# Attention and SwiGLU in one kernel: who makes which sum when

## The chip, the cores and the metric

The kernel runs on one NeuronCore of a Trainium2 chip. Its engines work side by side, each through its own queue in order: TensorE (PE) multiplies, VectorE (DVE), ScalarE (ACT) and GpSimd (POOL) work on elements, and SyncE (SP) issues nearly all DMA transfers. The metric is the device time of one execution in microseconds, as the median of several runs.

## The reference

Two blocks in a row. All arithmetic is in f32; the four FFN weights are handed over in f64.

```python
q_n, k_n = rmsnorm(q, g_q), rmsnorm(k, g_k)          # 8 batches, 12 heads, 448 x 64
scores = q_n @ k_n.T / sqrt(64)
attn = exp(scores - max) / (sum + 1e-9)
x = (attn @ v)   # heads side by side: 3584 tokens x 768
xn = x / sqrt(mean(x * x) + 1e-6) * rms_g
out = (silu(xn @ w_gate) * (xn @ w_val)) @ w_out     # 768 -> 1536 -> 768
```

## The kernel before

**Tiling.** Attention goes by pairs of heads: g runs from 0 to 47, six pairs to each of the eight batches b. While pair g's scores, exponentials and weighted values are made, the FFN of the batch before is fed in between them in small items. The program is written out by hand in order: `pe(fn)` emits one step of TensorE work, counts it in `now["t"]`, and then emits what was put off with `after(n, fn)` to that step. `fill()` takes FFN items from `todo`, as many as are due by cost, and after each emits side work on VectorE: a weight conversion (`convert`), a left sum (`slow`, `first_sums`), and sums of weights (`derive`, `derive_o`, `derive_q`). So an instruction's place in its engine's queue is set by the step in which it was emitted.

**FFN as fast matrix products.** Batch 0 multiplies plainly (`plain`, L1590) while the f64 weights are converted to f32 in 72 pieces; each piece passes through load, `split` (two ScalarE instructions, L907 and L908), `join` (three VectorE instructions, L913 to L915), an add on GpSimd (L964) and a store to DRAM (L952). From batch 1 on, gate and value products use a scheme of 15 products in place of 18 for each 2x3 by 3x3 block product (`PRODUCTS`, `product`, matmuls at L1182), in four groups of columns (`GROUPS`). Its left operands are sums of x (`LEFT_G`), its right operands are raw weight blocks (b11 to b33) or combined ones (v1 to v14, `RIGHT_G`). Nine combined blocks per group, 36 in all, are made once, during batch 1, by `derive` with one or two VectorE instructions each (L1087, L1090), used at once, and stored to DRAM, from where later batches load them. Twenty-four sums of output weights (`derive_o`, L1122) and 21 sets of further sums (`derive_q`, L1150 to L1153) are made beside it in batches 1 and 2. For batches 2, 5 and 6 the output projection (`out_quads`, L1518) runs a scheme of products inside products; its left sums are made by `left_q1` (L1392) and `left_sums` (L1364).

**Places.** Weight blocks live in one arena of 66 units: blocks of four units for gate and value ("wg"), of three for the output weights ("w"). Batch 1's gate blocks ("wg1") can also lie in six buffers that the conversion no longer needs. While sets of `derive_q` are outstanding, 18 units are set apart for the blocks that `derive_o` and `derive_q` read. `ask` walks the list of loads in order and issues the next one only if more than `keep_free` places would be left: six for batch 1's gate blocks, three otherwise, one around the first gate blocks of batch 2. `derive` needs one place for its result and its sources loaded some steps before. If a product's combined block is not there, `fill` forces the sum first. `block` picks the place that was freed longest ago, the lowest at a tie. `give_back` frees a place one step after its last use, three steps for "wg1".

**The steps that the change touches.**

- Pair 7 (g == NPAIR + 1) opens the overlapped part. `rms_x(0)` sums squares over x with four small matmuls (L726), after GpSimd's last addition (L644), and takes the root on VectorE and GpSimd (L728, L730). `norm_x(0)` spreads the result over partitions (L738) and scales the six chunks of x (L744).
- In each later even pair, the first step begins with `totals(g - 1)`: matmuls for the softmax denominators (L692), copies on ScalarE (L696, L699), reciprocals on VectorE. Its banks come from the same set of four as those of the scores (L659).
- `norm_x(b)` puts its six scalings off to later steps: two to a step, three in batch 1.
- In q1, the tenth product of a group, batches 2, 5 and 6 make three of the left sums of their output projection (`left_q1`) in the last group.

The lines of `ask` and `block` at issue are these:

```python
            kind, keep_free = "wg" if key[0] == "wg" else "w", 3
            if key[1] == 1 and key[0] == "wg":
                kind, keep_free = "wg1", 6
...
        span = min(places(kind), key=lambda span: (max(freed[i] for i in span), span[0]))
```

Of the kernel before, what the change touches and what calls it, by code (L numbers as in the profile page):

```python
# [18 lines left out]
B, H, S, D = 8, 12, 448, 64  # L19
# [316 lines left out]
def safe_scores(  # L336
# [37 lines left out]
    st = {}  # L374
# [4 lines left out]
    def after(n, fn):  # L379
        due.append((now["t"] + n, fn))  # L380
# [351 lines left out]
    def norm_x(b):  # L732


        rs = st.pop(("rx", b))
        ps = (ps_s if b else ps_f).tile([128, 512], F32, name="rb", tag="s" if b else "f")
        for t in range(NT):
            nc.tensor.transpose(ps[:, t * P:(t + 1) * P], rs[:, t:t + 1].to_broadcast([P, 128]), ident[0:P, 0:P])  # L738

        whole = st["x", b]  # L740

        def scale(hp):
            x = whole[:, hp, :]
            nc.vector.scalar_tensor_tensor(x, x, rg[:, hp:hp + 1], ps[:, 0:S], ALU.mult, ALU.mult)  # L744

        for hp in range(NPAIR):
            if b:
                after(hp // (3 if b == 1 else 2), lambda hp=hp: scale(hp))
            else:
                scale(hp)  # L750
        if b == 0:
            return

        parts = st.pop(("x", b)).rearrange("p (h c) n -> p h c n", h=2)
        a = st["left", b] = {f"a{i + 1}{k + 1}": parts[:, :, k, i * HT:(i + 1) * HT] for i in range(2) for k in range(3)}

        def place(name):
            if name in OVER:
                return a[OVER[name]]
            if name in MADE[:4]:  # L760
                t = s_pool.tile([128, S], F32, name="xs")
            elif name in ("S2", "S0"):
                t = l2_pool.tile([128, S], F32, name="l2")
            else:
                t = more_x[("S4", "S5", "S13").index(name)]
            return t.rearrange("p (h n) -> p h n", h=2)

        def op(name):
            first, second, what = LEFT_G[name]
            one, two = a[first], a[second]  # L770
            a[name] = place(name)
            nc.vector.tensor_tensor(a[name], one, two, what)

        slow.extend((name, lambda name=name: op(name)) for name in MADE)
        st["x_at"] = now["t"]
# [88 lines left out]
        return [span for span in spans if None not in [freed[i] for i in span]]  # L864

    def block(kind="w"):
        span = min(places(kind), key=lambda span: (max(freed[i] for i in span), span[0]))
        for i in span:
            freed[i] = None
        if span[0] in spare:  # L870
            return spare[span[0]], span
        return arena[:, span[0] * 128:span[-1] * 128 + 128], span
# [165 lines left out]
    def ask():  # L1038

        if turn_of["n"] < TURNS:  # L1040
            return
        while side and (room(1, "side") or side[0][0] == "wd" and asked["derived"] > 32 and room(4, "wg")):
            key = side.pop(0)
            asked[key] = now["t"]
            st[key] = block("side" if room(1, "side") else "wg")
            nc.sync.dma_start(out=data(key), in_=home(key))
        while asked["n"] < len(uses):
            key = uses[asked["n"]]
            kind, keep_free = "wg" if key[0] == "wg" else "w", 3
            if key[1] == 1 and key[0] == "wg":  # L1050
                kind, keep_free = "wg1", 6
            elif asked["derived"] < len(derived):
                return
            elif asked["n"] in next_gate:
                keep_free = 1
            if key[0] == "wo" and key[2][0] == "T" and ("kept", *key[2:]) not in asked:
                return
            if key[0] == "wq" and asked.get("sums_q", 0) < KG * (key[2] + 1):
                return
            if not room(keep_free + 1, kind):  # L1060
                return
            asked["n"] += 1
            asked[key] = now["t"]
            st[key] = block(kind)
            src = home(key)
            nc.sync.dma_start(out=data(key)[:, 0:src.shape[-1]], in_=src)
# [103 lines left out]
        after(3 if key[0:2] == ("wg", 1) else 1, ask)  # L1170


    def product(b, g, left, right, onto=None):

        a = st["left", b]
        while left not in a:
            slow.pop(0)[1]()
        bank = ps_f.tile([128, 512], F32, name="ff", tag="f") if onto is None else onto
        key = ("wg", b, g, right)
        for w in range(2):  # L1180
            for c in range(2):
                nc.tensor.matmul(bank[:, w * HT:(w + 1) * HT], lhsT=data(key)[:, (2 * w + c) * 128:(2 * w + c + 1) * 128],  # L1182
                                 rhs=a[left][:, c, :], start=onto is None and w == c == 0, stop=c == 1, skip_group_check=True)
        done_with(key)
        return bank

    def three(b, n):
# [11 lines left out]
        def plus(name, ps):  # L1199
            nc.vector.tensor_tensor(T[name], ps[:, 0:S], T[name], ALU.add)  # L1200
# [56 lines left out]
        def q7(make):  # L1257
            onto("c11", make(bank["B"]), "d", ALU.subtract)

        def q2(make):  # L1260
            plus("c11", make(bank["X"]))

        def q0(make):
            onto("c23", make(bank["Y"]), "s")

        def q1(make):
            plus("c21", make(bank["B"]))
            if n == len(GROUPS) - 1 and in_quads(b):
                left_q1(b, 0, range(3))

        def q14(make):
            plus("c12", make(bank["X"]))
# [355 lines left out]
    LEFT = 10  # L1628
    todo, part = [], {"all": 0.0, "spent": 0.0, "slot": 0, "slots": 1}

    def fill(n=None):

        if n is None:
            part["slot"] += 1
            upto = part["all"] * min(part["slot"] / part["slots"], 1.0)
            n = 0
            while n < len(todo) and part["spent"] + todo[n][0] / 2 < upto:
                part["spent"] += todo[n][0]
                n += 1
        for _ in range(min(n, len(todo))):  # L1640
            _, turns, sums_made, fn = todo.pop(0)
            while turn_of["n"] < turns:
                if not convert():
                    pe(idle)
            made, key = sums_made or (0, None)
            while asked["derived"] < made or (key and key not in st):
                before = dict(asked)
                derive(0)
                if key and key[0] == "wo":
                    derive_o(0)  # L1650
                ask()
                if before == asked:
                    pe(idle)
            pe(fn)
            convert()

            if first_sums:
                first_sums.pop(0)()
            elif slow and now["t"] != st.get("no_x") and now["t"] - st["block"] > 4 and now["t"] - st["x_at"] >= NPAIR and may_make(slow[0][0]):
                slow.pop(0)[1]()  # L1660
            if 2 < now["t"] - st["block"] < 5:
                derive()
            if now["t"] - st["block"] > 4 and now["t"] != st.get("left_sums"):
                made = 0
                while made < 2:
                    done = derive()
                    if not done:
                        break
                    made += done
                for _ in range(0 if made else 2):  # L1670
                    derive_o()
                derive_q()

    def idle():
        pass
# [101 lines left out]
    for g in range(NG + 1):  # L1777
# [51 lines left out]
        if g == NPAIR + 1:  # L1829
            some = lambda *parts: [exps(g, i, scores(g, i)) for i in parts]  # L1830
            pe(lambda: (rests(g), some(0, 1)))
            pe(lambda: rms_x(0))
            pe(lambda: values(g - 1))
            pe(lambda: some(2, 3))
            pe(lambda: norm_x(0))
            pe(lambda: some(4, 5))
            pe(lambda: sums(g - 1))
            later_sums(g, 2)
            begin(0, 15)
        else:  # L1840
            sums_due = g % 2 == 0
            pe(lambda: (totals(g - 1) if sums_due else None, step(g, 0)))
            pe(lambda: [step(g, i) for i in (1, 2)])
            pe(lambda: [step(g, i) for i in (3, 4)])
            pe(lambda: ([step(g, i) for i in (5, 6)], weigh(g - 1, 2) if sums_due else hold(g - 1)))
            if g < NG:
                later_sums(g, 2)
        st["block"] = now["t"]
        after(2, lambda g=g: load_v(g + 2))
        if hp:  # L1850
            fill()
            norm_k(g + 1, 0)
            squares(g + 2, 0)
            squares(g + 2, 1)
            pe(lambda: turn(g + 1, 0))
            norm_k(g + 1, 1)
            some_rests(g)
            fill()
            pe(lambda: turn(g + 1, 1))
            fill()  # L1860
            continue
        fill(3)
        norm_k(g + 1, 0)
# [53 lines left out]
```

## Time and profile before

| | |
|---|---|
| median of 3 runs | 1528.84 us (1526.25 to 1530.41) |
| the profiled execution | 1526.52 us, its span 1524.7 us |
| granted TensorE clock | 0.994 in the mean |
| busy: ACT, POOL | 604, 741 us |
| DMA, mean | 212 GB/s |
| matmuls of the gate and value products, the largest group | 254.0 us in 1272 instructions of 353 ns |
| sums of exponentials on GpSimd (L714) | 253.1 us in 205 instructions of 1235 ns |

"Busy" is the time in which an engine has an instruction running. A row of the timeline or of the groups names the line, the engine, the operation, the tile written and those read, the shape and a count; what stands in brackets is the idle time of the engine just before it and the instruction that ended that idle time. PEld is the weight load, which runs beside the matmuls. The granted clock is 1.00 at full speed.

### The profile page before, as it was taken

What the parts mean: (1) busy time and instruction counts of PE and PEld (TensorE: products, weight loads), DVE (VectorE), ACT (ScalarE), POOL (GpSimd) and SP (SyncE); (2) the same over time, 40 slices, a digit from 0 to 9 for tenths busy, and PEclk for the clock granted to TensorE, in tenths of its full rate; (3) what the DMA queues carried; (4) which work ended last, traced back from release to release, by engine and by line L of the source; (5) the groups of instructions that cost most, each with busy time, mean ns of one, the idle gap of its engine ahead of it and who ended that gap; (6) DMA issues with size and microseconds to landing.
All of it is one profiled execution on the core that took longest, in us unless ns stands there. A gap on an engine that the chain in (4) does not pass through costs nothing.

```text
span 1524.7 us, 25730 instructions
## 1 busy us (share of the span) xinstructions
PE 1483.0 (97%) x8732; PEld 1157.2 (76%) x8732; DVE 1043.9 (68%) x1826; ACT 603.8 (40%) x1377; POOL 740.5 (49%) x708
## 2 busy tenths in 40 slices
PE   8999999998989999999999999999999999999997
PEld 4344445677755788887988789758788789899996
DVE  5777999697864687974569655635668655674674
ACT  6856765343322444225442444444542443101100
POOL 6967987656433363463544644345645632021002
PEclk9999999999999999999999999999999999999998
DMA  7758675776577899895557855575457755597675
GB/s 190 227 164 233 187 235 174 219 248 196 185 237 226 277 309 324 261 305 188 179 150 243 252 180 154 171 234 178 143 156 248 225 159 145 157 299 224 167 231 178
DMA packets 302176, 322.51 MB, mean 212 GB/s; under 512 B 81620, under 2 KB 243668, under 8 KB 302036
## 3 DMA queue, kind: packets, MB, share of 16 engines
q1 hardware_dynamic: 301108, 320.58, 68.6%
q8 instruction: 72, 1.18, 0.3%
q14 instruction: 68, 0.56, 0.1%
q10 hardware_dynamic: 800, 0.20, 0.1%
q0 software_dynamic: 128, 0.00, 0.0%
HBM read 266.90 MB, written 53.77 MB: 210 GB/s over the span
## 4 chain that ended last, share of the span: by engine, by line
PE 87%; DVE 8%; DMA 1%; issue 1%; SPq 1%; ACT 1%; POOL 0%; DVEq 0%; POOLq 0%; ACTq 0%
PE ff L1182 38%; PE ff L1518 14%; PE sc L659 8%; PE av L674 7%; PE ff L1590 6%; PE ff L1447 5%; PE ff L1320 2%; PE tr L545 2%; PE den L692 1%; PE den L607 1%; PE sc L563 1%; DVE l L1392 1%; PE av L590 1%; DVE w L1122 1%; DVE ms L496 1%
## 5 line engine op out<-in xcount | busy, mean ns | idle before, releaser
L714 POOL TENSOR_TENSOR es<-es,e 128x448 f32<-128x448 f32 x205 | 253.1, 1235 | 13.6
L1182 PE MATMUL ff<-x,w 128*128 128x224 f32 x1272 | 254.0, 353 | 1.4 <-DVE pb L1203 1.1
L1182 PEld LDWEIGHTS ff<-x,w 128*128 128x128 f32 x1272 | 238.5, 190 | 4.2 <-DVE pb L1203 1.4
L659 PE MATMUL sc<-qT,kT 64*64 64x448 f32 x1176 | 231.6, 539 | 1.8 <-ACT rd L699 1.8
L674 PE MATMUL av<-e,vt 64*64 64x448 f32 x984 | 193.3, 538 | 0.0
L664 ACT ACTIVATE e<-sc 128x448 f32<-128x448 f32 x294 | 155.1, 547 | 76.0 <-PE sc L659 59.6
L1182 PE MATMUL ff<-xs,w 128*128 128x224 f32 x848 | 168.4, 353 | 2.4 <-DVE w L1087 1.3
L1182 PEld LDWEIGHTS ff<-xs,w 128*128 128x128 f32 x848 | 158.6, 190 | 6.1 <-issue 3.4
L644 POOL TENSOR_TENSOR ss<-ss,rd 128x448 f32<-128x448 f32 x40 | 46.8, 1170 | 210.2 <-ACT rd L643 210.2
L709 POOL TENSOR_TENSOR es<-e 128x448 f32<-128x448 f32 x41 | 48.6, 1185 | 193.7 <-ACT e L664 193.7
L659 PEld LDWEIGHTS sc<-qT,kT 64*64 64x64 f32 x1176 | 78.9, 132 | 83.8 <-issue 61.0
L1518 PE MATMUL ff<-w,l 128*128 128x192 f32 x630 | 118.1, 328 | 4.9 <-DVE pa L1553 3.5
L1203 DVE TENSOR_TENSOR pc<-ff,l 128x448 f32<-128x448 f32 x56 | 34.9, 623 | 122.8 <-PE ff L1182 91.5
L515 POOL TENSOR_TENSOR rs<-ms,mhalf 128x12 f32<-128x12 f32 (+1 forms) x50 | 116.2, 2324 | 4.2
L1590 PE MATMUL ff<-x,w 128*128 128x448 f32 x288 | 111.8, 541 | 0.0
L1518 PEld LDWEIGHTS ff<-w,l 128*128 128x128 f32 x630 | 103.8, 190 | 10.2 <-DVE pa L1553 4.7
L674 PEld LDWEIGHTS av<-e,vt 64*64 64x64 f32 x984 | 66.1, 133 | 41.3 <-issue 41.3
L1200 DVE TENSOR_TENSOR pb<-ff,pb 128x448 f32<-128x448 f32 x84 | 52.3, 623 | 62.9 <-PE ff L1182 53.5
L1590 PEld LDWEIGHTS ff<-x,w 128*128 128x128 f32 x288 | 53.3, 190 | 51.1 <-issue 47.6
L1182 PE MATMUL ff<-top_x,w 128*128 128x224 f32 x424 | 89.4, 361 | 2.1 <-DVE w L1090 2.1
L1182 PEld LDWEIGHTS ff<-top_x,w 128*128 128x128 f32 x424 | 80.2, 193 | 13.4 <-issue 9.5
L1182 PE MATMUL ff<-l,w 128*128 128x224 f32 x432 | 86.5, 353 | 0.0
(210 smaller groups left out, 2820.2 us busy)
## 6 DMA issues: line engine op xcount, KB each, us to landing
w<-kept SPq DMA_DIRECT2D x383, 256.0 KB, 3.5
w<-kept_q SPq DMA_DIRECT2D x350, 192.0 KB, 3.7
w<-kept_o SPq DMA_DIRECT2D x150, 192.0 KB, 4.0
kept_q<-w SPq DMA_DIRECT2D x63, 192.0 KB, 3.6
qk<-in_q_dram SPq DMA_DIRECT2D x48, 192.0 KB, 3.9
qk<-in_k_dram SPq DMA_DIRECT2D x96, 96.0 KB, 3.9
raw<-in_moe_w_gate_dram SPq DMA_DIRECT2D x24, 384.0 KB, 4.7
raw<-in_moe_w_val_dram SPq DMA_DIRECT2D x24, 384.0 KB, 4.4
```

What stands on the lines that cost most here:

```text
L515: nc.gpsimd.tensor_tensor(st["rs", g][:, cols], ms, mhalf[:, cols], ALU.pow)
L644: after(m, lambda: (nc.gpsimd.tensor_tensor(ss, ss, rd, ALU.add), st.update({("summed", b): hp})))
L659: nc.tensor.matmul(ps[r, 0:S], lhsT=st["kT", g][r, keys_of(i)], rhs=st["qT", g][r, :], start=True, stop=True)
L664: nc.scalar.activation(e, ps[:, 0:S], ACT.Exp)
L674: nc.tensor.matmul(st["av", g][own(j), 0:S], lhsT=vt, rhs=st["e", g, i][r], start=i == 0, stop=i == PARTS - 1, skip_group_check=True)
L709: nc.gpsimd.tensor_tensor(st["es", g], st["e", g, 0], st["e", g, 1], ALU.add)
L714: nc.gpsimd.tensor_tensor(st["es", g], st["es", g], st["e", g, i], ALU.add)
L1182: nc.tensor.matmul(bank[:, w * HT:(w + 1) * HT], lhsT=data(key)[:, (2 * w + c) * 128:(2 * w + c + 1) * 128], rhs=a[left][:, c, :], start=o ...
L1200: nc.vector.tensor_tensor(T[name], ps[:, 0:S], T[name], ALU.add)
L1447: nc.tensor.matmul(ps, lhsT=left_o(b, which, LEFT_O[name], c), rhs=data(("wo", b, name, c)), start=first and c == 0, stop=c == NFP - 1, sk ...
L1518: nc.tensor.matmul(ps, lhsT=a[:, j, :], rhs=data(key)[:, n % 2 * HW:(n % 2 + 1) * HW], start=start and j == 0, stop=j == KG - 1, skip_grou ...
L1590: nc.tensor.matmul(bank[w][:, 0:S], lhsT=data(key)[:, c * 128:(c + 1) * 128], rhs=st["x", 0][:, 3 * half + c, :], start=half == c == 0, st ...
```

## The change

Six edits, none of which changes what is computed.

- Pair 7: `values(g - 1)` comes before `rms_x(0)`, and the fourth and fifth parts of the scores come before `norm_x(0)`.
- The last `fill` of an odd pair (`hold=True`) leaves out the conversion after its last item and notes it in `st["held"]`; the conversion is emitted after the next pair's first step, the one with the totals.
- Loads of batch 1's gate blocks leave four places, not six, once the first nine combined blocks are made.
- `soon()`: while the second group's combined blocks are made (more than 9 and fewer than 18), `fill` makes no sum of this kind and none of the output weights in a step if it made one in each of the two steps before and the next one is due more than five products ahead (`LEAD`). `product` notes where batch 1 stands (`st["made"]`, `place_of`).
- `block` picks, for three-unit blocks and while `derive_q` sets are outstanding, the highest place among those freed two steps ago or earlier; if there is none, the one freed longest ago.
- The left sums of q1 are spread: the first comes at q2, the second at q0, the third at q1. In the last batch, `norm_x` puts its scalings one to a step.

```diff
-                after(hp // (3 if b == 1 else 2), lambda hp=hp: scale(hp))
+                after(hp // (3 if b == 1 else 1 if b == B - 1 else 2), lambda hp=hp: scale(hp))
...
-        span = min(places(kind), key=lambda span: (max(freed[i] for i in span), span[0]))
+        last = lambda span: max(freed[i] for i in span)
+        order = lambda span: (last(span), span[0])
+        if kind == "w" and count["done"] and todo_q:
+            order = lambda span: (max(last(span), now["t"] - 2), -span[0])
+        span = min(places(kind), key=order)
...
-                kind, keep_free = "wg1", 6
+                kind, keep_free = "wg1", 4 if asked["derived"] >= len(RIGHT_G) else 6
...
+    def place_of(g, right):
+        return GROUPS.index(g) * len(PRODUCTS) + [name for _, _, name in PRODUCTS].index(right)
+
     def product(b, g, left, right, onto=None):
 
+        if b == 1:
+            st["made"] = place_of(g, right)
...
+        def first_left(at):
+            if n == len(GROUPS) - 1 and in_quads(b):
+                left_q1(b, 0, (at,))
+
         def q2(make):
             plus("c11", make(bank["X"]))
+            first_left(0)
 
         def q0(make):
             onto("c23", make(bank["Y"]), "s")
+            first_left(1)
 
         def q1(make):
             plus("c21", make(bank["B"]))
-            if n == len(GROUPS) - 1 and in_quads(b):
-                left_q1(b, 0, range(3))
+            first_left(2)
...
-    def fill(n=None):
+    def fill(n=None, hold=False):
...
             pe(fn)
-            convert()
+            if hold and not left_over:
+                st["held"] = True
+            else:
+                convert()
...
-                made = 0
-                while made < 2:
+                made, rest = 0, soon()
+                while made < 2 and not rest:
                     done = derive()
                     if not done:
                         break
                     made += done
-                for _ in range(0 if made else 2):
+                if made:
+                    st["derived at"] = (st.get("derived at", (0, 0))[1], now["t"])
+                for _ in range(0 if made or rest else 2):
                     derive_o()
                 derive_q()
+
+    def soon():
+
+        if not len(RIGHT_G) < asked["derived"] < 2 * len(RIGHT_G):
+            return False
+        g, to = derived[asked["derived"]]
+        return st.get("derived at") == (now["t"] - 2, now["t"] - 1) and place_of(g, to) > st.get("made", 0) + LEAD
+
+    LEAD = 5
...
             pe(lambda: (rests(g), some(0, 1)))
+            pe(lambda: values(g - 1))
             pe(lambda: rms_x(0))
-            pe(lambda: values(g - 1))
             pe(lambda: some(2, 3))
+            pe(lambda: some(4, 5))
             pe(lambda: norm_x(0))
-            pe(lambda: some(4, 5))
             pe(lambda: sums(g - 1))
...
             pe(lambda: (totals(g - 1) if sums_due else None, step(g, 0)))
+            if st.pop("held", None):
+                convert()
...
-            fill()
+            fill(hold=g % 2 == 1)
```

More of the change, by code (lines that the diff above doesn't have):

```diff
@@ L1639, in fill @@
                 n += 1
-        for _ in range(min(n, len(todo))):
+        for left_over in reversed(range(min(n, len(todo)))):
             _, turns, sums_made, fn = todo.pop(0)
```

## The prediction

> **What bounds the kernel.** I read the page first: TensorE is busy nearly throughout, and in the chain that ended last its own work has 87%, VectorE's 8%.
>
> ```profile
> span 1524.7 us, 25730 instructions
> PE 1483.0 (97%) x8732; PEld 1157.2 (76%) x8732; DVE 1043.9 (68%) x1826; ACT 603.8 (40%) x1377; POOL 740.5 (49%) x708
> ```
>
> No matmul is removed or added by the change, so it can only win what TensorE idles or runs slowly. Second view: TensorE's waits.
>
> ```profile
> PE ff L1182 <- DVE pb L1200: 4.8, 3, 2.4
> PE ff L1518 <- DVE pa L1553: 3.5, 4, 2.0
> PE ff L1182 <- DVE raw L1090: 2.7, 3, 1.3
> PE ff L1182 <- DVE w L1090: 2.1, 1, 2.1
> ...
> PE ff L1447 <- DMA w<-kept_o: 1.9, 1, 1.9
> PE sc L659 <- ACT rd L699: 1.8, 1, 1.8
> ```
>
> Laid out in order of time with the timeline, TensorE's gaps sum to 31.3 us, the tail left out. 6.0 us lie in the start-up before 26 us and are not touched. Most of the rest sits where the change works: 86 and 92 us (0.69 + 0.73, rms_x and norm_x of the first batch), 213.7 us (1.79), the gate stage of batch 1 from 288 to 423 us (10.9) with 1.87 us behind it at 427 us, 612 us (2.03) and 1331.6 us (1.99). Third view: busy time in the four gate groups of batch 1 and around one gap (columns: stretch, length, busy of PE, PEld, DVE, ACT, POOL, granted clock, DMA).
>
> ```profile
> 288.00:319.00 31.00, 29.92 (x186) 25.36 (x185) 27.92 (x42) 12.75 (x31) 17.59 (x17) 1.00 0.75 239
> 319.00:352.00 33.00, 30.48 (x195) 25.68 (x194) 29.66 (x46) 15.38 (x37) 17.45 (x15) 1.00 0.76 248
> 352.00:387.00 35.00, 31.53 (x183) 26.24 (x183) 26.90 (x45) 12.53 (x28) 18.07 (x16) 0.95 0.57 183
> 387.00:423.00 36.00, 32.04 (x205) 26.59 (x204) 31.97 (x51) 14.15 (x32) 15.42 (x14) 1.00 0.58 190
> ...
> 359.50:362.90 3.40, 1.26 (x7) 0.94 (x7) 3.36 (x5) 0.53 (x1) 2.89 (x3) 1.00 0.85 278
> 362.90:366.30 3.40, 3.40 (x11) 3.08 (x10) 1.49 (x3) 0.53 (x1) 0.00 (x0) 0.50 0.98 291
> ```
>
> Two things are to be seen. The four groups do the same products, yet need 31, 33, 35 and 36 us, with VectorE busy 85 to 90% in each; and the 2.14 us gap at 359.9 is followed by 3.4 us at half clock, which costs another 1.7 us. The same view shows it again from 615.5 to 618.9 us, after the gap at 612.
>
> **The change, part by part.**
>
> *1. First batch, values moved ahead of rms_x, norm_x behind four parts of scores.* Same instructions. Before, rms_x waited 0.69 us for GpSimd's L644 (ends 87.09), and norm_x 0.73 us for L730 (ends 92.82). Now values (2.48 us) covers the first, and msx can start at about 88.9. VectorE's L728 is behind conversions that end at 91.65 in any order, so L730 still ends at 92.8; TensorE gets to norm_x at about 93.2. Both waits go: 1.4 us. What is late next: the first ff needs norm_x's six scalings (L744, 3.64 us), each product only its own slice, and the sums' 2.4 us still stand between. I take 1.3 (ends 0 and 1.4).
>
> *2. One conversion held back until after the totals (each odd pair).* The price is in one place:
>
> ```profile
> 213.29 0.56 ACT L907 ACTIVATE top_x<-raw 128x384 f32<-128x384 f32 x1 [1.48 <-POOL w L964]
> ...
> 214.32 1.06 ACT L699 COPY rd<-den 64x448 f32<-64x448 f32 x2
> ...
> 215.44 0.59 PE L659 MATMUL sc<-qT,kT 64*64 64x448 f32 x2 [1.79 <-ACT rd L699]
> ```
>
> ScalarE stood 1.48 us at a conversion's split, which waited for GpSimd, and the totals' copies stood behind it, holding the score banks. Moved behind them, the conversion's whole set (three VectorE, two ScalarE, one GpSimd, a load and a store on SP) comes one step later; weight blocks are made many blocks ahead of their use, so nobody waits for it. 1.7 us (ends 0 and 1.8). VectorE is busy 48.7 of the 50 us from 200 on, so up to 1 us of parts 1 and 2 may be handed back there; I subtract 0.6.
>
> *3. Batch 1's gate stage: loads leave four places, group-two sums rest each third step, out-weight blocks taken from the high end.* These belong together. From the timeline, a combined weight's last sum ended only 0.15, 0.05, 0.15, 0.05, 0.15, 0.05 and 0.06 us before its product's first matmul (v10, v13 of group two; v4, v11 of three; v9, v14, v11 of four):
>
> ```profile
> 345.96 1.50 DVE L1090 TENSOR_TENSOR raw<-raw,w 128x512 f32<-128x512 f32 x1
> ...
> 347.61 1.75 PE L1182 MATMUL ff<-x,raw 128*128 128x224 f32 x8 [1.28 <-DVE raw L1090]
> ```
>
> In group one the sums led by 0.9 to 10.6 us. Stepping the old planner by its counters shows why: from step 174 on it turns down the next raw block with 5 or 6 places free, again and again; b22 and b13 of group two get in at steps 187 and 190, so v10 and v13 can't be made before 200 and 201, right at their products. With four left, two more blocks are in flight: b22 and b13 get in at about 176, and the sums come before the attention steps 193 to 197. Directly tied to late sums are 1.28 + 1.24 + 2.14 + 1.30 + 0.23 = 6.2 us; the 2.43 at 419 us is an eviction (L1200) queued behind four sums and two out-weight sums; the 1.87 at 427 us is a load behind six stores that wait for out-weight sums (SP L952, 5.82 us). Sums made earlier unload both.
>
> But VectorE's work isn't less: 116.5 us over 135. If TensorE gains 10 us, VectorE is at 93%. Groups one and two, at 90%, show 1.1 and 2.5 us of gaps. So I leave 5 us of the 10.9 standing: 5.9 won. Of the 1.87 I take half, 0.9. What the rests move (sums of 0.68 us, two per step) goes to steps with idle VectorE, such as 2.6 and 3.2 us at 364 and 372 us. The out-weight blocks' places are an operation the trace doesn't show: a place freed two steps ago makes SP wait for the matmul that last read it (SP L1066 <- PE L1182 is 249.5 us over 235 waits, 1.06 each, and today harmless); nearest row, so 0, ends +2 and -3.
>
> Here a rule weighs against the change. The Trainium skill (SBUF — State Buffer, "SBUF: two separate sides") says that a VectorE operation with two SBUF inputs and a GpSimd operation that reads SBUF lock each other out of a shared port for a whole instruction. The trace agrees in kind: L1090 takes 0.68 us alone and up to 1.56 while L714 or L709 runs. Sums moved earlier fall after other attention blocks, again into GpSimd's es sums. If all 10 instructions of five moved sums were hit, they would cost 10 x 0.85 = 8.5 us of VectorE and the gain would be near 0; by the row about a third of all sums are hit wherever they stand, the moved ones were themselves at 1.5 us, so I take no loss.
>
> The half clock: the skill (TensorE: Matmul & The Clock Gate, "Why this matters for your kernels") has the clock drop only past gaps of some 3 us. By that rule nothing is to be won, as no gap here is longer than 2.43. The trace says otherwise: 2.14 and 2.03 us inside one 3.4 us slice halve the next slice. So both drops go if these gaps shrink; 1.7 us each by the trace. I take 1.3 here (0.75 of it). Part 3: 5.9 + 0.9 + 1.3 = 8.1 us (ends -6 and +14).
>
> *4. Sums for batch 2's quarter product spread over q2, q0, q1.* At 605.2 us three L1392 take 0.55, 1.38 and 1.49 us in a row. VectorE idles 0.33, 0.89 and 0.89 us just before; with one sum in each, the first clear of GpSimd's L714, the chain to q13's bank (pb, L1200 at 613.57) is shorter by about 1.3 us: two derive_q quartets still stand in it. 1.3 plus 0.75 of the second clock drop (1.3) = 2.6; batches 5 and 6 have no gap there, 0. (Ends 0 and 3.7.)
>
> *5. Last batch, one scaling per step.* Three of the six L744 (0.63 each) leave the queue ahead of L1553, which TensorE awaits for 1.99 us: up to 1.6 won there. But VectorE runs without a break from 1324 to 1349 us, with 0.41 and 0.27 idle; the same scalings arrive three steps later, ahead of bb(2)'s operands. Net 0.4 (ends -0.5 and 1.6).
>
> **Sum.** 1.3 + 1.7 - 0.6 + 8.1 + 2.6 + 0.4 = 13.5 us. I round down to 12.5, since a queue this full never frees all of it. Span 1524.7 - 12.5 = 1512.2. The profiled execution took 1526.5, the median of the three runs is 1528.84, so 1516.3 on that scale.
>
> **Rivals.** *VectorE is the bound of the gate stage, not late sums.* For it: 85 to 90% busy, and no idle at all from 344.4 to 364.4 us, just where the gaps are. Against: 9 us idle between 364 and 405. Then part 3 gives 2 instead of 8.1, in all 7.4, rounded down by the same 1.0: 1522.4. Chance 0.25.
>
> *Places run out.* Raw blocks loaded sooner sit on places that the sums need; the old planner, with spare places used up, was down to 1 or 2 at steps 166 to 172 and once found none. If groups three and four meet that, each sum is made at its product. Nine more waits at the mean gap of the late sums (6.2 / 5 = 1.24 us) are +11.2, against 5.4 won in the other parts: 1534.6. It decides once the stage's gaps grow by more than 5.4. Against: at nearly every sum from step 180 on 5 to 7 places were free. Chance 0.10.
>
> *Parts cancel*: the gains of the early parts are returned at the next full VectorE queue and part 3 gives little: 1526. Chance 0.10. *Everything falls into place*, 17 us or more: 1511 or less, 0.08. The forecast has 0.47.
>
> **Numbers.** Range 1511 to 1526: forecast, first rival, and the edge of the cancelling case. 0.3% (4.6 us) is about what a measurement of this kernel tells from no change. Faster, below 1524.3: 0.47 + 0.08 + 0.24 of the first rival's 0.25 = 0.79; slower, above 1533.4: 0.09; same: 0.12.
>
> **What would show it.** No L699 wait at 213 us; leads of over 1 us for v10 and v13 of group two; the third and fourth groups at 32 to 33 us like the first; granted clock 1.00 in all slices between start and tail. Wrong if VectorE's share in the gate stage stays below 90% with gaps as before, or if SP's load queue shows new TensorE waits at L1182 for `w<-kept` that didn't exist.

## The result and the profile after

| | before | after |
|---|---|---|
| median | 1528.47 us, 6 runs | 1515.03 us, 6 runs |
| ratio, with its 95% interval | | 0.9916 [0.9903, 0.9928] |
| again, on another chip | 1526.47 us, 17 runs | 1515.99 us, 6 runs: 0.9934 [0.992, 0.9947] |
| profiled execution, its span | 1526.52, 1524.7 us | 1515.81, 1514.0 us |
| granted clock, mean | 0.994 | 0.997 |
| TensorE's gaps, without the tail (some 10 us behind its last matmul) | 31.3 us | 25.5 us |

The change makes the kernel some 10 to 13 us faster. The page of the changed kernel, first its span and the busy time of the engines:

```profile
span 1514.0 us, 25709 instructions
PE 1478.8 (98%) x8732; PEld 1154.0 (76%) x8732; DVE 1037.7 (69%) x1826; ACT 602.2 (40%) x1377; POOL 741.3 (49%) x708
```

TensorE and VectorE execute as many instructions as before; VectorE's busy time fell by 6 us, 2.8 of them in the sums of weights. TensorE's waits in the changed kernel (total us, times, longest):

```profile
PE ff L1461 <- DMA w<-kept_o: 3.6, 1, 3.6
PE ff L1191 <- DVE pb L1209: 3.2, 2, 2.4
PE ff L1532 <- DVE pa L1567: 1.7, 4, 0.5
PE ff L1191 <- issue: 1.6, 1, 1.6
...
PE ff L1191 <- DVE pc L1212: 1.4, 2, 1.1
...
PE ff L1191 <- DMA w<-kept: 1.3, 1, 1.3
PE ff L1532 <- DVE l L1406: 1.3, 2, 1.1
PE ff L1532 <- DMA w<-kept_q: 1.3, 1, 1.3
```

The lines have moved: products stand at L1191 (before L1182), their evictions at L1209 and L1212 (L1200, L1203), the sums at L1091 and L1094 (L1087, L1090), output products at L1461 and L1532 (L1447, L1518), the first of a set of `derive_q` at L1154 (L1150). Two things are to be seen. The waits for sums (`raw L1090`, `w L1090`, `w L1087`) and for `rd L699` are gone; in the gate stage one wait for an eviction is new (`pc L1212`, 1.07 us at 327) and one is longer (the row `issue`, 1.63 us at 348, 0.87 before). And the wait for `kept_o`, 1.9 us before, now leads the list at 3.6 us. Busy time by stretch (columns as before), the four gate groups, roughly cut, and what comes behind them:

```profile
284.00:313.60 29.60, 28.52 (x179) 24.13 (x178) 26.98 (x40) 11.97 (x30) 16.76 (x17) 1.00 0.77 246
313.60:346.40 32.80, 31.73 (x203) 27.10 (x202) 30.55 (x51) 16.03 (x39) 16.38 (x16) 1.00 0.78 255
346.40:377.50 31.10, 29.12 (x181) 24.47 (x181) 30.22 (x46) 12.29 (x28) 20.04 (x19) 1.00 0.57 185
377.50:411.60 34.10, 31.71 (x205) 26.82 (x204) 31.91 (x52) 14.15 (x32) 15.16 (x14) 1.00 0.66 219
...
415.80:419.20 3.40, 0.77 (x3) 0.45 (x4) 3.37 (x7) 0.00 (x0) 0.00 (x0) 1.00 0.96 302
419.20:422.60 3.40, 3.40 (x7) 1.89 (x7) 3.30 (x7) 0.48 (x1) 0.00 (x0) 0.50 1.04 363
```

From the first matmul of each group's products to that of the next group (in the last, to its end), the groups took 31.1, 32.9, 35.3 and 36.0 us before and take 31.1, 31.2, 31.8 and 33.9 us now. They keep clock 1.00, with VectorE at 97 and 94% in the third and fourth. Then TensorE stands, and the next slice runs at half clock. The same matmul in both traces tells where the time came from (after minus before, in us, summed up from the start):

| at, in the trace of before | shift | what lies between |
|---|---|---|
| 24 | -1.65 | a half-clock slice at 7.9 us, in the trace of before only; not the change |
| 95 | -3.30 | pair 7 |
| 215 | -5.24 | the totals |
| 254 | -4.49 | 0.75 given back |
| 414.5 | -11.77 | gate stage: 7.3 won |
| 431 | -8.26 | `kept_o` wait and half clock: 3.5 lost |
| 586 | -7.15 | wait for a load of `kept`, 1.30 at 577 |
| 654 | -9.05 | left sums, and a half-clock slice gone |
| end | -10.70 | last batch 0.9, the tail 0.75 |

The first row is no work of the edits, which all lie behind it: in both traces TensorE waits for its first loads until 7.12 us, and what differs is the clock behind that wait. So the change's own part of the 10.7 us is 9.05 us. A second trace of the changed kernel, which has such a slice at 7.7 us too, spans 1515.4 us, 9.3 less than before.

### The profile page after: what moved, and what is told of

Same layout as the page of the kernel before. It is cut to its first block, busy times and chain, and to the rows that moved or that the text cites. A ratio compares the mean times of both kernels' runs of the same rounds, so it can differ in the third digit from the quotient of the medians.

```text
span 1514.0 us, 25709 instructions
## 1 busy us (share of the span) xinstructions
PE 1478.8 (98%) x8732; PEld 1154.0 (76%) x8732; DVE 1037.7 (69%) x1826; ACT 602.2 (40%) x1377; POOL 741.3 (49%) x708
## 4 chain that ended last, share of the span: by engine, by line
PE 84%; DVE 8%; DMA 3%; issue 1%; SPq 1%; POOL 1%; ACT 0%; DVEq 0%; POOLq 0%
PE ff L1191 37%; PE ff L1532 13%; PE sc L659 7%; PE av L674 7%; PE ff L1604 6%; PE ff L1461 5%; PE tr L545 2%; PE den L692 1%; PE den L607 1%; PE sc L563 1%; PE av L590 1%; PE ff L1334 1%; DVE l L1406 1%; DMA w<-kept 1%; DVE w L1091 1%
## 5 line engine op out<-in xcount | busy, mean ns | idle before, releaser
L1191 PE MATMUL ff<-x,w 128*128 128x224 f32 x1296 | 259.6, 353 | 1.4 <-DVE pb L1212 1.1
L714 POOL TENSOR_TENSOR es<-es,e 128x448 f32<-128x448 f32 x205 | 253.4, 1236 | 13.6
L1191 PEld LDWEIGHTS ff<-x,w 128*128 128x128 f32 x1296 | 242.7, 190 | 5.4 <-DVE pb L1212 1.4
L1191 PE MATMUL ff<-xs,w 128*128 128x224 f32 x832 | 165.0, 353 | 2.9 <-issue 1.6
L1191 PEld LDWEIGHTS ff<-xs,w 128*128 128x128 f32 x832 | 155.7, 190 | 6.2 <-issue 3.0
L644 POOL TENSOR_TENSOR ss<-ss,rd 128x448 f32<-128x448 f32 x40 | 47.1, 1178 | 207.2 <-ACT rd L643 206.5
L709 POOL TENSOR_TENSOR es<-e 128x448 f32<-128x448 f32 x41 | 49.2, 1200 | 192.3 <-ACT e L664 192.3
L1532 PE MATMUL ff<-w,l 128*128 128x192 f32 x630 | 117.8, 328 | 3.7 <-DVE pa L1567 1.7
L515 POOL TENSOR_TENSOR rs<-ms,mhalf 128x12 f32<-128x12 f32 (+1 forms) x50 | 115.9, 2319 | 4.2
L1212 DVE TENSOR_TENSOR pc<-ff,l 128x448 f32<-128x448 f32 x56 | 34.8, 622 | 115.7 <-PE ff L1191 80.9
L1532 PEld LDWEIGHTS ff<-w,l 128*128 128x128 f32 x630 | 103.8, 190 | 8.7 <-DVE pa L1567 2.9
L1604 PEld LDWEIGHTS ff<-x,w 128*128 128x128 f32 x288 | 53.3, 190 | 51.1 <-issue 48.2
L1191 PE MATMUL ff<-top_x,w 128*128 128x224 f32 x440 | 91.1, 356 | 0.0
L1209 DVE TENSOR_TENSOR pb<-ff,pb 128x448 f32<-128x448 f32 x84 | 52.3, 623 | 56.1 <-PE ff L1191 50.3
L1191 PEld LDWEIGHTS ff<-top_x,w 128*128 128x128 f32 x440 | 81.8, 190 | 11.3 <-issue 8.5
L1191 PE MATMUL ff<-l,w 128*128 128x224 f32 x416 | 83.6, 353 | 1.1 <-DVE pc L1212 1.1
```

Source lines behind the costliest of these rows:

```text
L515: nc.gpsimd.tensor_tensor(st["rs", g][:, cols], ms, mhalf[:, cols], ALU.pow)
L644: after(m, lambda: (nc.gpsimd.tensor_tensor(ss, ss, rd, ALU.add), st.update({("summed", b): hp})))
L709: nc.gpsimd.tensor_tensor(st["es", g], st["e", g, 0], st["e", g, 1], ALU.add)
L714: nc.gpsimd.tensor_tensor(st["es", g], st["es", g], st["e", g, i], ALU.add)
L1532: nc.tensor.matmul(ps, lhsT=a[:, j, :], rhs=data(key)[:, n % 2 * HW:(n % 2 + 1) * HW], start=start and j == 0, stop=j == KG - 1, skip_grou ...
L1604: nc.tensor.matmul(bank[w][:, 0:S], lhsT=data(key)[:, c * 128:(c + 1) * 128], rhs=st["x", 0][:, 3 * half + c, :], start=half == c == 0, st ...
```

## The experiments

Each kernel was timed in five rounds beside the kernel before on the same chip.

### Four parts, each alone on the kernel before

*Pair 7 alone.*

```diff
+            pe(lambda: values(g - 1))
             pe(lambda: rms_x(0))
-            pe(lambda: values(g - 1))
             pe(lambda: some(2, 3))
+            pe(lambda: some(4, 5))
             pe(lambda: norm_x(0))
-            pe(lambda: some(4, 5))
```

> The kernel before with the new order of pair 7 alone. Theory (a wait that TensorE has is simply covered): the gaps of 0.69 us before msx and 0.73 us before rb go, and 1.4 us stay won to the end: ratio 0.999. Rival (the next full VectorE queue takes it back): the gaps go, but the gap before the totals' scores at 213.7 us grows from 1.8 to about 3.2 us and the time is unchanged.

Measured: 1522.76 against 1525.79 us, 0.9978 [0.9968, 0.9989]. In its trace both waits (0.69, 0.73) are gone and no gap replaces them before 210 us; 0.40 us are given back at 252. That is 1.0 to 1.4 us, and the medians say 3.0. So it was run a second time, with the question whether the rest was spread.

> The kernel before with the order of pair 7 alone, again. The gaps of its first trace explain 1.4 us, less 0.4 given back; the medians gave 3.0. If the rest was the spread of runs and clock: ratio 0.9985 to 0.9995. If something that the gaps don't show comes with the order: 0.997 to 0.998 once more.

Measured: 0.9985 [0.9975, 0.9994], some 2.3 us, at the edge of what spread alone was to give. The trace again has these two gaps gone. It shows 0.60 us at 253.7, where the first one has 0.40, and 2.30 us at 585.2 that the first one doesn't have, with the same instructions in the same order. Both measurements, 2.3 and 3.0 us, lie above the 1.0 to 1.4 that the gaps account for. The second one's interval (0.9 to 3.8 us) covers these, the first one's doesn't; what makes up the rest stays open.

*The held conversion alone.*

```diff
-            convert()
+            if hold and not left_over:
+                st["held"] = True
+            else:
+                convert()
...
-            fill()
+            fill(hold=g % 2 == 1)
```

> The kernel before with the held-back conversion alone. Theory: the 1.79 us before the scores at 213.7 us go; a first batch's end that is full of VectorE work gives about 0.7 us back near 250 us, so 1.1 us are won: ratio 0.999. Rival: all of it comes back near 250 us, since VectorE is busy 48.7 of 50 us there: 1.000.

Measured: 1524.29 us, 0.9993 [0.9982, 1.0004]. The 1.79 us before the scores at 213 are gone, and 0.71 stands before those at 252.5: net 1.1 us in the trace, 1.5 in the medians, inside the interval of no change.

*The gate stage alone: four places, rests, the high end.*

```diff
-        span = min(places(kind), key=lambda span: (max(freed[i] for i in span), span[0]))
+        last = lambda span: max(freed[i] for i in span)
+        order = lambda span: (last(span), span[0])
+        if kind == "w" and count["done"] and todo_q:
+            order = lambda span: (max(last(span), now["t"] - 2), -span[0])
+        span = min(places(kind), key=order)
...
-                kind, keep_free = "wg1", 6
+                kind, keep_free = "wg1", 4 if asked["derived"] >= len(RIGHT_G) else 6
...
-                made = 0
-                while made < 2:
+                made, rest = 0, soon()
+                while made < 2 and not rest:
```

> The kernel before with the three edits of batch 1's gate stage alone (four places, rests, high places). Theory (late sums): the five gaps of 6.2 us at late sums go, and the clock drop at 363 us; but the output projection's first blocks come later and cost a new wait of about 3.6 us with its own clock drop: 3 to 5 us won, ratio 0.997 to 0.998. Rival (VectorE is the bound): gaps of the same sum return elsewhere in the stage, under 2 us won.

Measured: 1520.03 us, 0.9957 [0.9942, 0.9971], 5.8 us. All five gaps at late sums and the half-clock slice at 363 are gone, worth 7.2 us at 414 us; the `kept_o` wait is 3.51 us in place of 1.87, with a half-clock slice behind it. So the loss behind the stage belongs to this part and not to the others.

*The left sums alone.*

```diff
         def q2(make):
             plus("c11", make(bank["X"]))
+            first_left(0)
...
         def q1(make):
             plus("c21", make(bank["B"]))
-            if n == len(GROUPS) - 1 and in_quads(b):
-                left_q1(b, 0, range(3))
+            first_left(2)
```

> The kernel before with the left sums spread over q2, q0 and q1 alone. Theory: the gap at 612 us shrinks from 2.03 to about 0.8 us and the clock drop at 615.5 us goes, together 2.5 to 3 us: ratio 0.998. Rival (the drop is not bound to this gap): 1.2 us won and the drop stays: ratio 0.999.

Measured: 1524.44 us, 0.9991 [0.9981, 1.0002]. The gap at 613.6 us is 0.92 instead of 2.03 and the half-clock slice behind it is gone, 2.8 us. 1.20 us of waiting for a load of `kept` stand at 586, ahead of the edited steps, so they can't come from the edit; pair 7 alone has nothing or 2.30 us before this product, in two executions of one program (the profile puts the 2.30 down to L1153, a sum of `derive_q`). In the medians 1.4 us, inside the interval of no change.

The four gains, 3.0 + 1.5 + 5.8 + 1.4 = 11.7 us, add up to the change's own within its spread, though two of them can't be told from zero one by one.

### Single edits undone in the changed kernel

*Six places again.*

```diff
-                kind, keep_free = "wg1", 4 if asked["derived"] >= len(RIGHT_G) else 6
+                kind, keep_free = "wg1", 6
```

> The changed kernel with six places left again. Theory (the two further places are what makes sums early): v10 and v13 of group two are made at steps 200 and 201 again, the waits at late sums return, and nearly all that the gate stage gave is lost: 5 to 7 us slower than the changed kernel, ratio to before 0.995 to 0.996. Rival (the rests and the high places do it): at most 2 us slower, ratio 0.992 to 0.993.

Measured: 1519.53 against 1524.97 us, 0.996 [0.9945, 0.9976]. TensorE's waits in this kernel show the late sums back, one for one:

```profile
PE ff L1191 <- DVE raw L1094: 2.7, 3, 1.3
PE ff L1191 <- DMA w<-kept: 2.4, 1, 2.4
PE ff L1191 <- DVE w L1094: 2.1, 1, 2.1
PE ff L1461 <- DMA w<-kept_o: 1.9, 1, 1.9
...
PE ff L1191 <- DVE w L1091: 1.3, 1, 1.3
```

At 410 us it is 7.2 us behind the changed kernel. 1.7 of these are there at 24 us already, before any edit acts, so that the stage itself costs 5.5. Behind the stage 3.4 come back at once, as the `kept_o` wait is again 1.9 us and has no half-clock slice behind it. So loading sooner wins 5.5 us in the stage (7.3 against the kernel before, whose 2.14 us gap also halved a slice) and pays more than half of it at its end. The medians, 4 to 7 us behind the changed kernel by the ratios, hold more than what is then left, and the trace shows where it comes about: a load wait of 2.38 us at 581 with a half-clock slice behind it, and two of 1.20 and 0.67 us at 620 and 653.

*No rests.*

```diff
-                made, rest = 0, soon()
+                made, rest = 0, False
```

> The changed kernel without the rests. Stepping the planner shows one single rest in the whole kernel, at step 186. Theory (one sum of 1.4 us moved by one step): the evictions near 325 us wait a little longer, 0 to 1 us; but the output weights' fourth block then comes at step 248 instead of 242, and the wait at the first output products is as long as now or up to 1 us longer: ratio 0.9916 to 0.993. Rival (the rest carries the gate stage): 3 us or more slower, 0.9935 and up.

Measured: 1518.98 us, 0.9958 [0.9945, 0.9972], some 4 to 6 us behind the changed kernel by the ratios. The counters of `fill`, stepped by hand, give a surprise: in the whole program `soon()` is true once, at step 186. The timeline of this kernel at that place (start, length, engine, line, operation):

```profile
329.23 0.69 DVE L1091 TENSOR_TENSOR w<-raw,w 128x512 f32<-128x512 f32 x1
...
329.94 1.20 DVE L1094 TENSOR_TENSOR w<-w 128x512 f32<-128x512 f32 x1
331.07 0.61 DVE L1212 TENSOR_TENSOR pc<-ff,l 128x448 f32<-128x448 f32 x1
...
331.73 1.59 PE L1191 MATMUL ff<-l,w 128*128 128x224 f32 x7 [2.90 <-DVE pc L1212]
```

And of the changed kernel:

```profile
327.24 0.69 DVE L1094 TENSOR_TENSOR w<-w 128x512 f32<-128x512 f32 x1
327.85 0.62 DVE L1212 TENSOR_TENSOR pc<-ff,l 128x448 f32<-128x448 f32 x1
...
328.52 1.78 PE L1191 MATMUL ff<-l,w 128*128 128x224 f32 x8 [1.07 <-DVE pc L1212]
329.12 0.68 DVE L1091 TENSOR_TENSOR raw<-raw,w 128x512 f32<-128x512 f32 x1
```

Without the rest one more sum, 0.69 + 1.20 us, stands ahead of an eviction that TensorE waits for: 2.90 against 1.07 us. One rest puts that sum behind the eviction. The trace also has a second half-clock slice: 6.8 us of half clock from 419.5 on, 3.4 in the changed kernel. Part of that is won back, and 1.4 us of this trace's lag are there before any edit acts. So of the medians' 4 to 6 us only these 1.8 are settled.

*The old choice of places.*

```diff
-        if kind == "w" and count["done"] and todo_q:
-            order = lambda span: (max(last(span), now["t"] - 2), -span[0])
```

> The changed kernel with the old choice of places. By the planner, the first six output blocks come at the same steps either way. Theory (the place matters only for SP's waits, which are hidden): the same time within 1 us, ratio 0.991 to 0.9925. Rival (high places keep room for the gate blocks of batch 2): the loads near 540 to 590 us come late and 2 to 4 us are lost, ratio 0.993 to 0.9945.

Measured: 1523.03 us, 0.9982 [0.997, 0.9994]: of the change's gain 1.9 us are left. Up to 415 us its gaps are those of the changed kernel. Most of the loss, 6.2 us, stands at 616 to 660 us, in the quarter products of batch 2 (timeline of this kernel):

```profile
634.64 5.52 SPq L1162 DMA_DIRECT2D kept_q<-w  x3
...
637.42 1.28 DVE L1152 TENSOR_TENSOR w<-w 128x192 f32<-128x192 f32 x1
...
640.16 1.24 PE L1530 MATMUL ff<-w,l 128*128 128x192 f32 x6 [1.66 <-DVE pb L1565]
...
642.13 4.20 SPq L1068 DMA_DIRECT2D w<-kept_q  x9
...
645.06 1.27 PE L1530 MATMUL ff<-w,h 128*128 128x192 f32 x6 [2.02 <-DMA w<-kept_q]
```

Sets of `derive_q` still run here (L1152 there): their VectorE instructions stand ahead of an eviction, and their stores hold SP for 5.5 us, with nine loads behind them. All instructions of that line, first in the changed kernel, then in this one (name, count, ns, first and last start in us):

```profile
L1154 DVE TENSOR_TENSOR w<-w x21: 343/351/1286, 442.0 to 608.7; 128x192 f32<-128x192 f32 x21
```

```profile
L1152 DVE TENSOR_TENSOR w<-w x21: 348/352/1284, 487.9 to 647.6; 128x192 f32<-128x192 f32 x21
```

The same 21 sets come 46 us later at the front and 39 at the end. Why can be read from the counters: a set needs two whole four-unit places. With the old choice the three-unit blocks lie scattered, and from step 252 to step 288 just one four-unit place is whole; the first set goes in at step 289. With blocks taken from the high end two are whole at steps 263 and 269, and two sets go in there. The two that the old choice put off are made last, at steps 390 and 395, in the middle of the products that read them. The kernel before, with the old choice too, had two sets in at steps 266 and 269: where the holes fall depends on the order of all that came before. So the new choice wins nothing over that kernel; it keeps away a loss that the other edits would bring. Undoing the four places or the rests moves these sets too (they run from 451.9 to 626.6 and from 452.1 to 618.3 us), so not all that those two runs lose behind the stage is owed to the sums.

*Two scalings per step in the last batch again.*

```diff
-                after(hp // (3 if b == 1 else 1 if b == B - 1 else 2), lambda hp=hp: scale(hp))
+                after(hp // (3 if b == 1 else 2), lambda hp=hp: scale(hp))
```

> The changed kernel with two scalings per step in the last batch again. Theory (VectorE is full there and hands back most of it): the gap of 2 us at about 1322 us returns, the one of 1.1 us at 1331 us goes, net 0.5 to 1 us slower, with now and then a clock drop: ratio 0.992. Rival (the whole 1.8 us stay won): 0.9928.

Measured: 1515.52 us, 0.9936 [0.9919, 0.9952], not to be told from the changed kernel. In its trace the wait of 1.99 us at 1320 is back and the one of 1.10 at 1331 gone: 0.9 us.

### The wait at the end of the gate stage

The timeline of the changed kernel shows how the largest wait comes about:

```profile
412.04 2.76 PE L1461 MATMUL ff<-w,top 128*128 128x384 f32 x8
...
412.68 1.97 SPq L956 DMA_DIRECT2D kept_o<-w  x4
...
414.69 2.18 SPq L1070 DMA_DIRECT2D w<-kept_o  x4
...
418.43 2.19 PE L1461 MATMUL ff<-w,top 128*128 128x384 f32 x4 [3.63 <-DMA w<-kept_o]
```

The first of these loads issued at 414.69 are blocks 4 and 5 of the first output products. The counters say that they were turned down from step 242 on with three places free, where three must stay, and let in at step 249, behind four stores. In the kernel before, the same counters let block 4 in at step 245 and only block 5 at 250, and its TensorE runs ten of these matmuls, not eight, before it waits:

```profile
423.75 3.40 PE L1447 MATMUL ff<-w,top 128*128 128x384 f32 x10
...
429.03 0.91 PE L1447 MATMUL ff<-w,top 128*128 128x384 f32 x2 [1.87 <-DMA w<-kept_o]
```

> The changed kernel again, as the reference for the runs beside it: ratio to before 0.990 to 0.993, and the same gaps (2.4 us at 407, 3.6 us at 415). If its clock slices fall elsewhere, up to 1.7 us of difference for each in the profiled execution.

This is the changed kernel again on another chip: 1515.99 us, 0.9934 [0.992, 0.9947], with the same two waits (2.40 at 409.6, 4.03 at 416.7). Beside it ran two kernels with one and two edits more.

```diff
-            elif asked["n"] in next_gate:
+            elif asked["n"] in next_gate or key[0:3] == ("wo", 1, "B11"):
                 keep_free = 1
```

> The changed kernel with one more edit: the first output-weight blocks of batch 1 may leave one place instead of three, so that blocks 4 and 5 are loaded at step 242 and not at 249. Theory 1 (the wait of 3.6 us at 415 us is this refusal: two loads issued behind stores that wait for output-weight sums): the wait and the half-clock slice behind it go, 3.6 + 1.7 us, of which up to 2 may come back later; 3.3 to 5.3 us faster than the changed kernel, ratio to before 0.988 to 0.9895. Theory 2 (the queue of VectorE, full to 91-97% in these groups, is the bound and the wait only shows where it runs out): the wait turns into waits of the same sum on VectorE; within 1.5 us of the changed kernel.

Measured: 1511.79 us (1510.02 to 1512.56), 0.991 [0.9897, 0.9923]; the changed kernel beside it 1513.66 to 1517.31. That is 4.2 us less, and no run of one reaches the other's. Windows of this kernel over the same stretch:

```profile
415.80:419.20 3.40, 3.40 (x12) 1.95 (x11) 3.37 (x7) 0.48 (x1) 0.00 (x0) 1.00 1.00 315
419.20:422.60 3.40, 3.40 (x31) 1.31 (x33) 3.30 (x8) 1.71 (x4) 0.26 (x1) 1.00 1.03 369
```

TensorE runs through, at full clock. VectorE is as full as before (3.37 of 3.40 us) and no wait for it takes the place: the refusal was the cause, not the full queue. This version has the lowest median of all that were run.

The other wait, 2.39 us at 407, is an eviction (L1209) behind output-weight sums (L1126). The second edit keeps these sums off the two steps concerned:

```diff
-                for _ in range(0 if made or rest else 2):
+                for _ in range(0 if made or rest or st.get("made", 0) in (55, 56) else 2):
```

> The kernel of the run before with one edit more: no output-weight sum in the two steps that follow the last two combined weights' products, so that those sums don't stand ahead of the eviction that TensorE waits for at 407 us (2.39 us). If that queue is the cause, the gap shrinks to about 0.6 us, and it is 1 to 2 us faster than the run before. If the sums put off collide with the output projection's weights instead, new waits on VectorE at L1532 between 415 and 450 us take it back, 0 to 2 us slower than the run before.

Measured: 1515.16 us, 0.9928 [0.9913, 0.9943], slower by 3.4 us than with the first edit alone. The wait at 407 shrank to 0.27 us, so that its cause is right. The price came at a place that neither expectation named, 190 us later (timeline of this kernel):

```profile
593.47 1.59 SPq L1164 DMA_DIRECT2D kept_q<-w  x3
...
598.31 0.36 DVE L1154 TENSOR_TENSOR w<-w 128x192 f32<-128x192 f32 x1 [2.00 <-DMA kept_q<-w]
...
600.02 0.61 DVE L1209 TENSOR_TENSOR pb<-ff,pb 128x448 f32<-128x448 f32 x1
...
600.69 1.80 PE L1191 MATMUL ff<-raw,w 128*128 128x224 f32 x4 [3.40 <-DVE pb L1209]
```

A set of `derive_q` waits 2.00 us for a store that still reads the place it is to write, and VectorE, which works in order, lets the eviction behind it wait too: 3.40 us of TensorE, a half-clock slice, and 1.78 us at 609. In the run before the same wait was 1.2 us and TensorE's gap 2.12. What the second edit changes is what the old choice of places changed too: stepped by its counters, this kernel finds no two whole four-unit places at steps 263 and 269, its first set goes in at 290 and its last at 391. In its trace the instructions of L1154 run from 480.9 to 635.5 us, in the run before from 436.4 to 603.3. That the later sets make the waits longer is argued from this, not shown by a run of its own.

## Why the prediction was right, and where its steps were wrong

The sum was 12.5 us. The medians give 13.4 and, on the second chip, 10.5; the profiled pair 10.7, of which 9.05 are the change's. It is right in sign and in size, but not step by step. Its terms added up to 13.5, and the 4.4 us between that and 9.05 are as much as one step was wrong by, the one behind the gate stage; the other differences are small and cancel. That the medians come nearer to 12.5 than this is in part luck: what they have beyond the traces is not explained by any gap.

**Part 1 (1.3 us)** was right in mechanism: both waits went, nothing took their place. Its size came out larger, 2.3 to 3.0 us in the medians, and the gaps don't explain the difference.

**Part 2 (1.7 less 0.6)** was right in both halves. The stall at the totals went, and VectorE's full queue near 250 us took 0.71 back.

**Part 3, late sums (5.9, and 1.3 for the clock)** was right: 7.3 us won in the stage, against 7.2, with the new eviction wait of 1.07 us and the longer one already taken off. The leads (from the end of a sum to its product's first matmul) of v10 and v13 of group two went from 0.15 and 0.05 to 15.07 and 13.99 us, and no lead from group two on is below 5.1. The rule on the shared SBUF port (the Trainium skill, SBUF — State Buffer, "SBUF: two separate sides") would have allowed a loss of 8.5 us. The trace shows none: of the 60 instructions of the sums 13 took over 0.75 us, 16 before, and all of them together 47.7 us against 50.5. The traces also show which ones are hit. Each of these 29 long instructions started while GpSimd was at work on a tile of 192 to 448 columns (L714, L709, L644, L520, L469 and a copy), and each ended 0.54 or 0.55 us after that GpSimd instruction. Those that started first, or while GpSimd worked on 6 or 12 columns (L515 above all), took 0.70 us or less. The moved sums met GpSimd no less often, but mostly in such small instructions. That agrees with the page in that whoever starts first is not held up; in these traces the small instructions hold up nothing.

**Part 3, the 1.87 us behind the stage (0.9 won)** is the step that failed: "Sums made earlier unload both" held for neither. The eviction kept its 2.4 us: output-weight sums still stand ahead of it, as the run with both edits shows (0.27 us without them). The load wait grew to 3.63 us and cost a half-clock slice, together 3.5 us lost instead of 0.9 won. I took SP's stores as the cause and counted on their coming sooner. The cause was a refusal in `ask`: blocks turned down with three places free. The run that lets them in shows it, with 4.2 us.

**Part 3, the choice of places (0, ends +2 and -3)** was taken for nearly free, yet undone it costs 6.2 us in the trace and 7 to 10 in the medians. I priced the operation, a wait of SP for a freed place, and not what it decides, namely whether two whole four-unit places exist when `derive_q` asks. The figure belongs to the changed kernel. Against the kernel before, which has no such loss, nothing was won, so that the 0 in the sum did no harm; the choice alone on that kernel was not tried.

**Part 3, the rests**: I wrote of sums moved two per step; there is one rest in all, and it is worth 1.8 us at 331 us; a half-clock slice more came with its loss in the one trace of it.

**Part 4 (2.6)**: the wait at 605 us shrank by 1.2 us and the half-clock slice behind it went, as worked out. Alone it gave 1.4 us, less than these two together; the wait that comes and goes at 586 us may hide the rest (not shown). A wait for `w<-kept` at a product, named as a sign of trouble, did appear with 1.30 us, but before a product at which one program shows 0 or 2.30. **Part 5 (0.4)**: 0.9 us in the trace, by the mechanism named, one wait of 1.99 us exchanged for one of 1.10.

**The rivals.** VectorE as the bound fell: in groups two to four it is 93 to 97% busy, and the gaps at sums are gone all the same. What is left of gaps there are evictions. (The prediction gives VectorE 9 us of idle time between 364 and 405; the trace has 11.3, which speaks against this rival a little more.) Places didn't run out: at each sum of group two three or four were free. Parts didn't cancel. Of the signs two failed: clock 1.00 in all slices, at 419 us, and 32 to 33 us for the fourth group, which took 33.9.

## What to carry over

A list of loads with a fixed reserve of free places is a queue like an engine's: when a wait for a DMA stands at its head, look first for the step in which the load was refused, not for the store before it. Price a change of placement by who next needs a whole place, and step the planner through to the end of the consumers, for a gain in one stage may be paid 190 us later. And where one engine evicts for another in order, what counts is not how busy it is, but which instruction stands just ahead of the eviction: one sum moved behind it was worth 1.8 us.

## What was unexpected of the hardware

The half-clock slices are 3.41 us long and cost 1.7 us each, and whether a gap sets one off depends on where it falls. The same 2.14 us gap of the gate stage halves the next slice in the traces of before (at 362.9 us), of pair 7 alone in its first run (359.8), of the held conversion and of the left sums (both 362.5). It doesn't in the kernel with six places (gap at 357.06, no half-clock slice before 584.0) nor in the second run of pair 7 (gap at 358.76, none before 427.3). The two runs of pair 7 are one program, some us sooner or later.

The kept traces settle what decides. In each of them all changes of the clock lie whole multiples of 3.413 us apart, so the slices form a grid, and its place differs from execution to execution. Cut by that grid, the 14 traces have, the tail left out, 24 slices at full clock in which TensorE stood for 1.99 us or more: all 24 are followed by a half-clock slice. Of those in which it stood for less, only one is, with 1.92 us; two others with 1.92 and 1.93 are not. In the second run of pair 7 an edge of the grid, at 359.03 us, cuts the gap, so that 1.92 us fall into one slice; with six places the edge is at 358.71, and the larger part is 1.64 us. So here a gap of 2.0 to 2.4 us is harmless when an edge cuts it and costs 1.7 us when it doesn't. The Trainium skill (TensorE: Matmul & The Clock Gate, "Why this matters for your kernels") names gaps of some 3 us; in these traces 2.0 us inside one slice are enough.

This makes up much of the spread between runs. The runs of the kernel before beside these experiments, by granted clock: 0.994, mean 1527.6 us (21 runs); 0.995, 1525.2 (28); 0.996, 1524.2 (15). One half-clock slice more lowers the mean clock of 1525 us by 0.0011 and costs 1.7 us (an estimate from the slice's length), so two slices more or less are about the 3.4 us between the first and the last of these groups. That is as much as most of the edits here are worth. Gains of 1 to 2 us were therefore read from gaps in the traces.
